# Attention with top-32 selection and an ELU feed-forward: the first batch in single-tile blocks, and another order of the last queries in odd batches

## The chip, the cores and the metric

The kernel runs on one core of a Trainium2 chip. The metric is device time in microseconds (us) of one launch. Before the change, three runs took 1779.0, 1779.35 and 1781.24 us; the median is 1779.35. The engines are named as in the profile: PE is TensorE (matmuls and transposes), DVE is VectorE, ACT is ScalarE, POOL is GpSimd, SP issues the DMAs.

## The reference

There are 8 batches, 8 heads, 576 positions and 64 numbers per head. For each query the 32 largest scores are kept, a softmax is taken over them, and the result weighs the values. The output of all heads, 512 numbers per token for 4608 tokens, then goes through two matrices with an ELU between them.

```python
scores = scale * np.matmul(q, k.transpose(0, 1, 3, 2))
kth = np.partition(scores, -top_k, axis=-1)[..., -top_k:-top_k + 1]   # top_k = 32
mask = scores >= kth
scores = np.where(mask, scores, -1000000000.0)
attn = np.exp(scores - scores.max(-1, keepdims=True))
attn = attn / (attn.sum(-1, keepdims=True) + 1e-09)
x = np.matmul(attn, v)            # (B,H,S,D) -> (B*S, H*D) = 4608 x 512
h = x @ w_in                      # 512 x 2048
g = np.where(h > 0.0, h, np.exp(np.minimum(h, 0.0)) - 1.0)
return g @ w_out                  # 2048 x 512
```

The two weight matrices arrive as 64-bit floats and are turned into 32-bit ones on the chip. Everything else is in 32-bit floats.

## The kernel before, in words

**Tiles and steps.** The 576 queries of a batch are four tiles of 128 queries (numbers 0 to 3) and a rest of 64 (number 4, `J` in the code). A step treats one tile for one head pair, that is 128 queries of two heads. The rest takes four heads in one step, so that its 64 queries still fill 128 rows. A batch is 16 + 2 = 18 steps, and 8 batches are 144 steps. Lines 540 to 549 lay down the order: `order` lists which tiles go together (`(0, 1)` alternates tiles 0 and 1 for each head pair). Even batches go (0,1), (2,3), rest; odd batches go (0,1), rest, (2,3). In the first batch tiles 0 and 1 go singly.

**A step's work.** `scores` (line 274) multiplies keys and queries on PE, and ACT copies the result out. `select` and, for the first eight steps, `select_row` find the 32nd largest score on DVE with eight MAX8 and six MATCH_REPLACE8 per step. `mask` runs Prelu and Exp on ACT, with two small POOL operations before them; `normalise` has a reciprocal on DVE and two multiplications on POOL. `turn` transposes the weights on PE (nine transposes) and ACT copies them out as `et`. Once all tiles of a group are turned, `attend` (line 393) multiplies them with the values: for a pair of tiles 10 matmuls of 256 columns, for one tile 10 of 128, for the rest 20 of 64. `finish` copies the result into the transposed input `xT` of the feed-forward stage.

**The pipeline.** The loop of line 610 spreads a tile's work over steps. In iteration n it emits the scores of step n+2, the selection of n, the mask of n-1, the turning of n-2, and the attend of a group closed one iteration before. From step 8 on the instructions of PE, ACT, DVE and POOL stand in the order written (`manual_schedule`, line 636); before that, and always for SP's DMAs, a scheduler orders them. PE, ACT and DVE each take their instructions in that order.

**Keys, queries and values.** `load_qk` loads two heads' keys and queries, `transpose_qk` turns them with ten transposes on PE and three copies on ACT into `kqT`, and `load_v` loads the values. `ld` has two buffers for keys and two for queries; `kqT` and the values have five each, so a new batch takes over buffers of the old one one by one. Lines 561 to 568 say how many steps before (or, with a minus, after) the batch's first step `f` each of the four head pairs is loaded, turned, and its values loaded. For every batch that is `(7,5,2), (5,3,-2), (3,1,-2), (1,-1,-3)`.

**Feed-forward blocks.** Tokens are gathered into blocks over a pair of batches, nine tile slots in all, where the two rests of 64 share a slot. `division` (lines 517 to 519) gives the blocks: in the first pair (0), (1), (2,3), (rest), (4,5), (6,7), with numbers from 4 on for the odd batch; in later pairs (0,1), (2,3), (rest,4,5), (6,7). When a block's tokens are complete, `ffn_pieces` appends 16 hidden pieces (four matmuls each, then Relu and Exp on ACT, and a gate on DVE that makes the ELU) and four projection pieces for each slot (four matmuls of 512 columns each; the last also copies the result out and stores it). Hidden results pass through two buffers of PSUM, so the third waits for the first one's gate.

**Pacing.** `feed` (line 572) is called four times a step. It hands out pieces from the list in order, at a rate such that the work of all blocks known earlier is done when the next block becomes due. `due` (lines 547 to 554) holds each block's time of readiness, 2.5 steps after its last step, and the work of the blocks before it, in the planner's costs: `HIDDEN` is 1.1, 1.85 or 2.7 per hidden piece of one, two or three slots, `PROJECT` is 3.55 per projection piece. Pieces of later blocks wait until all weights are converted. `hook` (line 189) does a piece of the conversion at each call, four times in each of the first eight steps, and opens the pools `g` and `x` after the last piece. `x` holds `xT` of single-slot blocks from then on, with one buffer.

Of the kernel before, what the change touches and what calls it, by code (L numbers as in the profile page):

```python
# [80 lines left out]
def kernel(  # L81
# [13 lines left out]
    J = S // P  # L95
# [28 lines left out]
    late = {}  # L124
# [64 lines left out]
    def hook():  # L189

        if not decode:
            return
        decode.pop(0)()
        if not decode:
            raws.close()
            late["g"] = ctx.enter_context(tc.tile_pool(name="g", bufs=2))
            late["x"] = ctx.enter_context(tc.tile_pool(name="x", bufs=1))

    def decode_piece(i):
        if i < 2 * NF:  # L200
# [96 lines left out]
    def select_row(u, i):  # L297
        if i == 0:
            u.first = small.tile([P, 2, 8], FP32, tag="m1", name="m1")
            u.last = small.tile([P, 2, 8], FP32, tag="m4", name="m4")  # L300
        sc = u.sc[:, i, :]
        m = u.first[:, i, :]
        nc.vector.max(m, sc)
        wk = wkpool.tile([P, S], FP32, tag=f"wk{i}", name="wk")
        cur = sc
        for r in range(TOP_K // 8 - 1):
            nc.vector.match_replace(wk[:], m, cur, TAKEN)  # L307
            cur = wk[:]
            if r < TOP_K // 8 - 2:
                m = small.tile([P, 8], FP32, tag=f"m{i}", name="m")[:]  # L310
            else:
                m = u.last[:, i, :]
            nc.vector.max(m, cur)  # L313
            if r != 1:
                hook()
                yield

    def select(u):

        u.first = small.tile([P, 2, 8], FP32, tag="m1", name="m1")  # L320
        u.last = small.tile([P, 2, 8], FP32, tag="m4", name="m4")
        cur = [u.sc[:, i, :] for i in range(2)]
        found = [u.first[:, i, :] for i in range(2)]
        for i in range(2):
            nc.vector.max(found[i], cur[i])  # L325
        yield
        wk = [wkpool.tile([P, S], FP32, tag=f"wk{i}", name="wk")[:] for i in range(2)]
        for r in range(TOP_K // 8 - 1):
            for i in range(2):
                nc.vector.match_replace(wk[i], found[i], cur[i], TAKEN)  # L330
            cur = wk
            for i in range(2):
                if r < TOP_K // 8 - 2:
                    found[i] = small.tile([P, 8], FP32, tag=f"m{i}", name="m")[:]
                else:
                    found[i] = u.last[:, i, :]
                nc.vector.max(found[i], cur[i])  # L337
            hook()
            yield
# [174 lines left out]
    for b in range(B):  # L514
        if b % 2 == 0:
            rest = 2 * J
            division = [(0,), (1,), (2, 3), (rest,), (4, 5), (6, 7)]
            if b > 0:
                division = [(0, 1), (2, 3), (rest, 4, 5), (6, 7)]
            slots = {}  # L520
            for part in division:
                blk = Block(len(blocks), len(part))
                blocks.append(blk)
                slots.update((x, (blk, s)) for s, x in enumerate(part))
        first[b] = len(steps)
        tiles = []
        for qt in range(J + 1):
            r0 = b * S + (JP if qt == J else qt)
            if qt == J:
                (blk, slot), c0, n = slots[rest], (b % 2) * R, R  # L530
                rows = slice(r0, r0 + R)
            else:
                (blk, slot), c0, n = slots[(b % 2) * J + qt], 0, P
                rows = slice(r0, r0 + J * (P - 1) + 1, J)
            c0 += slot * P
            t = Tile(b, qt, rows, blk, slice(c0, c0 + n))
            blk.left += NHP
            blk.tiles[slot].append(t)
            tiles.append(t)
        order = [(0, 1), (2, 3), (J,)] if b % 2 == 0 else [(0, 1), (J,), (2, 3)]  # L540
        if b == 0:
            order[:1] = [(0,), (1,)]
        for qts in order:
            for hp in range(NHP // 2 if qts == (J,) else NHP):
                group = Group([tiles[qt] for qt in qts], hp)
                steps += [Step(tiles[qt], hp, group, i) for i, qt in enumerate(qts)]
            for qt in qts:
                n = len(steps)
                tiles[qt].block.ready = n + 1.0 if n <= tight else n + 2.5
# [8 lines left out]
    def at(step, fn, *args):  # L558
        todo.setdefault(step, []).append((fn, args))

    for b in range(1, B):
        f = first[b]
        for hp, (ahead, ready, late_v) in enumerate(
            ((7, 5, 2), (5, 3, -2), (3, 1, -2), (1, -1, -3))
        ):
            at(f - ahead, load_qk, b, hp)
            at(f - ready, start_qk, b, hp)
            at(f - late_v, load_v, b, hp)
# [36 lines left out]
    def step(n):  # L605
        return steps[n] if 0 <= n < NS else None

    closing = []
    main, rest, other = slice(0, J), slice(J, J + 1), slice(J + 1, 2 * J + 1)
    for n in range(NS + 3):  # L610
        for fn, args in todo.pop(n, []):
            fn(*args)
        ahead, cur, prev, done = step(n + 2), step(n), step(n - 1), step(n - 2)
# [86 lines left out]
```

## Time and profile before

| | before |
|---|---|
| median of three runs | 1779.35 us |
| profiled execution, its time | 1779.21 us |
| profiled execution, its span | 1777.4 us |
| PE busy | 1645.8 us (93%) |
| weight loads (PEld, beside PE) | 1014.2 us (57%) |
| DVE busy | 1549.9 us (87%) |
| ACT busy | 1140.0 us (64%) |
| POOL busy | 407.9 us (23%) |
| DMA | 56.19 MB, mean 32 GB/s |
| mean granted PE clock | 0.969 |

The span is the time from the first to the last instruction of the program, and the run's own time is 1.8 us longer. A matmul of the program shows as two MATMUL records, a transpose as one. Busy time on PE includes the tail of a pipelined matmul. The steps can be found in the trace by DVE's first MAX8 on new scores: step 8 starts at 144.22 us, step 20 at 267.89, step 36 at 436.52, step 72 at 844.27, step 140 at 1629.37, and the last, 143, at 1670.34.

### The profile page before, as it was taken

To read this page: it belongs to the slowest core of one execution; us is meant where nothing else is said; L and a number is where in the kernel's file an instruction comes from. 1 tells how busy PE (TensorE), PEld (TensorE's weight loads), DVE (VectorE), ACT (ScalarE), POOL (GpSimd) and SP (SyncE) were. 2 spreads that over 40 slices of the span, in tenths; PEclk is the share of its full clock that TensorE was granted. 3 is DMA by queue.
4 is the path that set the end of the run, shared out by engine and by line. 5 is a ranking of instruction groups with operands and counts; after the bars stand their busy time and mean duration, and the time that the engine had idled before them with its cause. 6 is when DMAs were issued, how large, how long until landed. Compare 5 with 4: busy or idle time off the path is not lost.

```text
span 1777.4 us, 25611 instructions
## 1 busy us (share of the span) xinstructions
PE 1645.8 (93%) x8352; PEld 1014.2 (57%) x8352; DVE 1549.9 (87%) x3376; ACT 1140.0 (64%) x2473; POOL 407.9 (23%) x1078
## 2 busy tenths in 40 slices
PE   5577899999899999999999999999999999999999
PEld 3354656475665666555556565655547475655565
DVE  7999999999899999988999898988889988997700
ACT  6785767676676766667666665756657575756521
POOL 3663222222222222221222122221222211221200
PEclk7568999999999999999999999999999999999999
DMA  6540011001100111001100011001110010000000
GB/s 169 169 131 25 20 47 28 13 18 44 34 7 7 33 34 33 3 19 33 47 12 1 26 38 43 1 13 41 26 27 7 12 29 27 7 6 7 7 13 12
DMA packets 101125, 56.19 MB, mean 32 GB/s; under 512 B 84096, under 2 KB 92288, under 8 KB 100992
## 3 DMA queue, kind: packets, MB, share of 16 engines
q1 hardware_dynamic: 100992, 54.55, 11.1%
q8 instruction: 67, 1.10, 0.3%
q14 instruction: 66, 0.54, 0.1%
HBM read 45.09 MB, written 9.44 MB: 31 GB/s over the span
## 4 chain that ended last, share of the span: by engine, by line
PE 64%; DVE 24%; ACT 6%; issue 2%; DMA 1%; POOL 1%; SPq 0%; ACTq 0%; POOLq 0%
PE ops L485 26%; PE hps L467 17%; DVE wk L330 9%; PE avps L410 8%; DVE m L337 8%; PE scps L285 7%; PE eps L383 5%; DVE m L325 2%; DVE gT L447 2%; ACT et L384 2%; DVE wk L307 1%; DVE m L313 1%; DMA raw<-in_moe_w_in_dram 1%; ACT n L476 1%; ACT n L475 1%
## 5 line engine op out<-in xcount | busy, mean ns | idle before, releaser
L467 PE MATMUL hps<-xT,w_in 128*128 128x256 f32 (+2 forms) x2304 | 563.2, 391 | 27.0 <-DVE gT L447 26.7
L337 DVE MAX8 m<-wk 128x8 f32<-128x576 f32 x816 | 575.8, 747 | 0.0
L485 PE MATMUL ops<-w_out,gT 128*128 128x512 f32 x1152 | 524.8, 600 | 0.6 <-DVE gT L447 0.6
L467 PEld LDWEIGHTS hps<-xT,w_in 128*128 128x128 f32 x2304 | 402.3, 194 | 127.4 <-DVE gT L447 36.0
L330 DVE MATCH_REPLACE8 wk<-m,wk 128x576 f32<-128x576 f32 x544 | 400.0, 743 | 0.0
L485 PEld LDWEIGHTS ops<-w_out,gT 128*128 128x128 f32 x1152 | 209.7, 191 | 221.0 <-issue 215.7
L363 POOL TENSOR_SCALAR dene<-den 128x2 f32<-128x2 f32 x144 | 32.8, 228 | 1062.1 <-ACT sc L354 1061.8
L383 PE MATMUL eps<-ident,sc 128*128 128x128 f32 x1296 | 209.7, 285 | 64.9 <-ACT et L384 33.1
L384 ACT COPY et<-eps 128x512 f32<-128x512 f32 (+1 forms) x432 | 191.0, 473 | 117.1 <-PE eps L383 116.5
L293 ACT ACTIVATE sc<-scps 128x576 f32<-128x576 f32 x288 | 171.9, 648 | 133.5 <-PE scps L285 132.9
L367 POOL TENSOR_SCALAR sc<-sc,rec 128x576 f32<-128x576 f32 x288 | 215.0, 757 | 172.8 <-DVE rec L365 145.3
L383 PEld LDWEIGHTS eps<-ident,sc 128*128 128x128 f32 x1296 | 157.6, 144 | 157.0 <-issue 73.3
L354 ACT ACTIVATE sc<-sc,gap 128x576 f32<-128x576 f32 x288 | 223.2, 775 | 25.2
L353 ACT ACTIVATE sc<-sc,neg 128x576 f32<-128x576 f32 x288 | 223.9, 778 | 22.6 <-POOL neg L350 22.5
L285 PE MATMUL scps<-kqT 64*128 64x512 f32 (+3 forms) x1280 | 203.6, 450 | 12.2 <-ACT sc L293 10.7
L475 ACT ACTIVATE n<-hps 128x256 f32<-128x256 f32 (+2 forms) x288 | 109.1, 379 | 163.9 <-PE hps L467 160.0
L410 PE MATMUL avps<-et,vT 128*64 128x256 f32 (+5 forms) x2000 | 201.5, 337 | 4.0 <-ACT et L384 3.9
L330 DVE MATCH_REPLACE8 wk<-m,sc 128x576 f32<-128x576 f32 x272 | 200.0, 743 | 0.0
L447 DVE SCALAR_TENSOR_TENSOR gT<-n,hps 128x256 f32<-128x256 f32 (+2 forms) x288 | 117.1, 408 | 91.1 <-ACT n L476 90.2
L325 DVE MAX8 m<-sc 128x8 f32<-128x576 f32 x272 | 191.4, 745 | 0.0
L285 PEld LDWEIGHTS scps<-kqT 64*128 64x128 f32 (+1 forms) x1280 | 108.8, 180 | 125.6 <-issue 102.8
L410 PEld LDWEIGHTS avps<-et,vT 128*64 128x64 f32 (+1 forms) x2000 | 113.0, 140 | 90.6 <-issue 50.4
(40 smaller groups left out, 834.5 us busy)
## 6 DMA issues: line engine op xcount, KB each, us to landing
kin<-in_k_dram SPq DMA_DIRECT2D x64, 128.0 KB, 2.8
qin<-in_q_dram SPq DMA_DIRECT2D x64, 128.0 KB, 2.7
raw<-in_moe_w_in_dram SPq DMA_DIRECT2D x16, 512.0 KB, 4.3
vT<-in_v_dram SPq DMA_DIRECT2D x64, 128.0 KB, 2.3
raw<-in_moe_w_out_dram SPq DMA_DIRECT2D x16, 512.0 KB, 3.3
out_dram<-osb SPq DMA_DIRECT2D x32, 256.0 KB, 2.2
kin<-in_k_dram SPq DMA_DIRECT2D x32, 32.0 KB, 2.5
qin<-in_q_dram SPq DMA_DIRECT2D x32, 32.0 KB, 2.5
```

The source lines that it names most:

```text
L285: nc.tensor.matmul(ps[rows, start[i] : start[i] + keys.stop - keys.start], kq[part, 1, q0 : q0 + u.t.ql], kq[part, 0, keys], start=True, s ...
L325: nc.vector.max(found[i], cur[i])
L330: nc.vector.match_replace(wk[i], found[i], cur[i], TAKEN)
L337: nc.vector.max(found[i], cur[i])
L353: nc.scalar.activation(sc, sc, AF.Prelu, bias=neg[:], alpha=STEEP)
L354: nc.scalar.activation(sc, sc, AF.Exp, bias=gap[:], accum_out=u.den[:, i : i + 1])
L367: nc.gpsimd.tensor_scalar(u.sc[:, i, :], u.sc[:, i, :], rec[:, i : i + 1], 1.0, ALU.mult, ALU.mult)
L383: nc.tensor.transpose(ps[:, c * P : (c + 1) * P], sc[:, c0 : c0 + P], ident[:])
L384: nc.scalar.copy(g.et[:, chunks, u.at, :], ps[:, 0 : n * P].rearrange("p (c q) -> p c q", c=n),)
L410: nc.tensor.matmul(ps[i * D : (i + 1) * D, cols], vt[rows, 2 * J if c == J else i * J + c, :], w, start=(c == 0), stop=(c == J),)
L467: nc.tensor.matmul(ps[:, 0:n_tok], w_in[:, i, f * P : (f + 1) * P], blk.xT[:, i, 0:n_tok], start=(i == 0), stop=(i == NC - 1),)
L485: nc.tensor.matmul(blk.o[:], blk.gT[f // NG][:, f % NG, s * P : (s + 1) * P], w_out[:, f, :], start=(f == 0), stop=(f == NF - 1),)
```

## The change

It has four parts. In the first pair of batches the block (2,3) becomes two blocks of one slot, (2) and (3), and tiles 2 and 3 of the first batch go one after the other, as tiles 0 and 1 do. In every odd batch the rest comes first, straight behind the rest of the even batch, so that the two rests of a pair stand in four consecutive steps. Because such a step needs two head pairs, the odd batches' keys and queries are loaded and turned on four consecutive steps before `f`, and their values later. The pool `x` gets a second buffer.

```diff
@@ hook
-            late["x"] = ctx.enter_context(tc.tile_pool(name="x", bufs=1))
+            late["x"] = ctx.enter_context(tc.tile_pool(name="x", bufs=2))
@@ blocks of a pair of batches
-            division = [(0,), (1,), (2, 3), (rest,), (4, 5), (6, 7)]
+            division = [(0,), (1,), (2,), (3,), (rest,), (4, 5), (6, 7)]
             if b > 0:
                 division = [(0, 1), (2, 3), (rest, 4, 5), (6, 7)]
@@ order of the steps
-        order = [(0, 1), (2, 3), (J,)] if b % 2 == 0 else [(0, 1), (J,), (2, 3)]
+        order = [(0, 1), (2, 3), (J,)] if b % 2 == 0 else [(J,), (0, 1), (2, 3)]
         if b == 0:
-            order[:1] = [(0,), (1,)]
+            order[:2] = [(0,), (1,), (2,), (3,)]
@@ loads and transposes of a batch
     for b in range(1, B):
         f = first[b]
-        for hp, (ahead, ready, late_v) in enumerate(
-            ((7, 5, 2), (5, 3, -2), (3, 1, -2), (1, -1, -3))
-        ):
+        plan = ((7, 5, 2), (5, 3, -2), (3, 1, -2), (1, -1, -3))
+        if b % 2 == 1:
+            plan = ((7, 5, 0), (6, 4, -2), (5, 3, -3), (4, 2, -3))
+        for hp, (ahead, ready, late_v) in enumerate(plan):
             at(f - ahead, load_qk, b, hp)
             at(f - ready, start_qk, b, hp)
             at(f - late_v, load_v, b, hp)
```

## The prediction

> **What bounds the kernel now.** I read the page's slices first, then its chain, then the busy time of stretches cut at step boundaries. A step is one of 144 (query tile, head pair) units; its boundary is the first MAX8 of its scores on DVE.
>
> Slices of the span, 44 us each: PE, DVE and the granted TensorE clock.
>
> ```profile
> PE   5577899999899999999999999999999999999999
> DVE  7999999999899999988999898988889988997700
> PEclk7568999999999999999999999999999999999999
> ```
>
> DVE is full from the start and idle in the last two slices; PE has holes only in the first five, where its clock is also often halved. The chain agrees, and its last pieces show what the end consists of:
>
> ```profile
> PE 64%; DVE 24%; ACT 6%; issue 2%; DMA 1%; POOL 1%; SPq 0%; ACTq 0%; POOLq 0%
> ...
> 1718.42 27.63 PE hps L467 x128
> 1746.05 27.48 PE ops L485 x64
> ```
>
> These two are also prices. A matmul is two records, so a 256-column hidden matmul costs 27.63/64 = 0.432 us and a projection matmul 27.48/32 = 0.859.
>
> Busy time by stretch (start:end, length, then PE, PEld, DVE, ACT, POOL, clock, DMA). Rows two to five are steps 8-19, 20-35, 36-71 and 72-139.
>
> ```profile
> 0.00:144.22 144.22, 91.30 (x416) 58.50 (x417) 124.12 (x242) 108.42 (x226) 83.31 (x120) 0.67 0.52 152
> 144.22:267.89 123.67, 105.38 (x650) 68.10 (x648) 122.60 (x279) 82.42 (x191) 28.03 (x82) 0.97 0.10 24
> 267.89:436.52 168.63, 159.85 (x888) 102.09 (x887) 165.25 (x368) 116.72 (x255) 37.78 (x112) 1.00 0.09 23
> 436.52:844.27 407.75, 389.27 (x2078) 245.39 (x2077) 377.82 (x836) 274.59 (x605) 85.34 (x253) 1.00 0.09 23
> 844.27:1629.37 785.10, 757.49 (x3812) 458.62 (x3811) 708.65 (x1549) 505.62 (x1085) 160.39 (x477) 1.00 0.08 21
> 1629.37:1777.43 148.06, 142.51 (x517) 81.53 (x515) 51.40 (x113) 52.27 (x114) 13.08 (x37) 1.00 0.03 9
> ```
>
> Steps 8-19 are DVE's (122.6 of 123.7); PE idles 18.3 us. From step 36 on PE sets the pace, with 3.5 to 4.5% of idle time between its dependent pieces. So the time is PE's work plus PE's idle time. The change can only win by putting feed-forward work (hidden, projection) into the idle 18.3 us.
>
> **What the Trainium skill says.** "Perfetto Trace Analysis", Identifying the Most-Contended Engine, warns that matmul busy time is a poor measure of distance from the limit. I use it only to compare two orders of nearly the same matmuls. "TensorE: Matmul & The Clock Gate", Part 1, says the array runs at half clock until a window of some 3.4 us was busy. This trace agrees: the mean grant is 0.67 before step 8 and 1.00 from step 20. The same page (Architectural detail) says ACT and DVE are strict first-in first-out. That is seen here where PE waits for a copy queued behind a mask:
>
> ```profile
> 1252.99 0.77 ACT L354 ACTIVATE sc<-sc,gap 128x576 f32<-128x576 f32 x1
> 1253.77 0.56 ACT L248 COPY kqT<-qkps 128x512 f32<-128x512 f32 x1
> 1254.47 0.45 PE L383 MATMUL eps<-ident,sc 128*128 128x128 f32 x1 [2.45 <-ACT kqT L248]
> ```
>
> **The change, part by part.** Its instruction lists are fixed before it runs, so I count them by step and multiply by prices fitted to PE's busy time over the steps from 22 on: hidden 0.244 / 0.441 / 0.672 us for 128 / 256 / 384 columns, projection 0.875, attend 0.26 (256) and 0.092 (64), the rest about 2.5 per step. They give 390.4 for steps 36-71, where the row shows 389.3. DVE prices are starts from one instruction to the next: MAX8 0.663, MATCH_REPLACE8 with its load 0.727, gate 0.204 / 0.32 / 0.471.
>
> 1. *Block (2,3) split.* 128 narrow hidden matmuls for 64 wide: 128x0.244 - 64x0.441 = +3.0 us. 80 narrow attend matmuls for 40 wide: at 0.15 each (half of the wide 0.26 is the floor; the measured 0.26 of the narrow ones, 16.8 us for 131 records, is partly at half clock and the ceiling) 12.0 - 10.4 = +1.6, bounds 0 and +10. Gates: 32x0.204 - 16x0.32 = +1.4 of DVE.
> 2. *Earlier work.* The pacing spreads the work known to be due. With (2), (3) and the last queries due at steps 14.5, 18.5 and 22.5 instead of 18.5 and 30.5, feed-forward work is 20 us ahead by step 20. But the same pacing gives it back: 17 us ahead after step 39, 3.0 us (just the split's cost) by step 65, and what is left from step 140 on is the same (127.8 us in both). The lead never reaches the tail.
> 3. *Sums by stage.* PE before/after: 105.1/123.6, 161.5/161.3, 390.4/374.8, 751.8/751.8, end 152.0/152.0. DVE: 122.8/124.3, 165.1/167.4, 375.7/372.5, 703.6/703.6. Measured time over the larger sum before: 1.007, 1.021, 1.045, 1.044. Steps 8-19 come into balance, so I take 1.034 there, a little above the 1.021 of the balanced steps 20-35, for the narrow gates' latency: 124.3x1.034 = 128.5, +4.8. Steps 20-35: 167.4x1.021 = 170.9, +2.3. Steps 36-71: 374.8x1.045 = 391.7, -16.1.
> 4. *Odd batches, last queries first.* Scores, transposes and attends move, their number stays; PE's sum for steps 72-139 is unchanged. But four head pairs are turned in four consecutive steps, and the scores of the second step need the pair turned just before: they wait for two ACT copies (0.57 and 0.27), possibly behind a pair of hidden activations (0.38 and 0.42), while PE has about 0.8 of its own (six transposes at 0.11 and the first score matmul). An estimate of 0.9 us for each of three odd batches, +2.7 (bounds 0, and 7.4 for the 2.45 seen above). In the first odd batch DVE covers it. Behind that matmul stand the step's attend and transposes, and behind those ACT's mask and DVE's reciprocal.
> 5. *DMAs.* The same transfers. Keys and queries are asked for two steps ahead of their transposes; 2.8 us to land against 20. The third pair's load waits for the first pair's transposes, still two steps early. Values land 2.3 us after the attend that frees their buffer, a step (10 us) before use. Next-batch key loads stand ahead of them in SP's queue, but wait for earlier transposes. Uncovered, each would cost 2.3-2.8. The second xT buffer costs nothing; without it (3) would wait for (2)'s hidden stage.
> 6. *Steps 0-7.* Same chain of decode and selection; step 6 gets 2.9 us more hidden work at a partly halved clock: +1 (0 to 4; a gain of 3 if the clock rises sooner).
>
> Sum: +4.8 +2.3 -16.1 +2.7 +1 = -5.3. The profiled run took 1779.21 for a span of 1777.4; 1777.4 - 5.3 + 1.8 = 1773.9, and the median stands 0.1 above that run: **1774**.
>
> **Rivals.**
> *A, likeliest (0.47): as summed,* 1774, own range 1766 to 1775.8. For it: in steps 41-49, where the sums nearly agree (93.0 PE, 92.6 DVE), the trace needs 93.4, so PE's backlog carries over steps.
> *B (0.20): the gain is eaten.* The stall in part 4 takes 2.45 us and the narrow stage 0.2 us a step more: within 0.2%, 1779. Narrow hidden work does cost idle time before: over steps 37-39, all of it narrow, 36 us hold 3.6 of PE waiting for gates,
>
> ```profile
> L467 PE MATMUL hps<-xT,w_in 128*128 128x128 f32 x128 | 16.7, 281 | 3.6 <-DVE gT L447 3.6
> ```
>
> *C (0.26): slower, no carry.* If every step lasts as long as the larger of its own two sums, steps 8-139 go from 1476.4 to 1482.1: +10.1 in 8-19, +0.4 in 20-35, -7.1 in 36-71, +2.2 after; with parts 4 and 6, +9.4: 1789. For it: the step-wise sums of before fit 36-71 as well (408.3 against 407.8). Against: they give 173.2 for steps 20-35, which took 168.6. It decides from the point where 36-71 give back less than about 7 us instead of 16.
> *D (0.07): full carry,* the early steps cost only 2 and 36-71 give 20: 1766 or less.
> That the change does nothing is excluded: the lists differ from step 6 on.
>
> **How the numbers follow.** A measurement of this kernel tells 0.2% (3.6 us) from no change. A and D are faster, 0.54; B same, 0.20; C slower, 0.26. For 8 in 10 the range leaves out the lower half of D and the upper half of C: 1763 to 1788.
>
> **What would show it.** Right: steps 8-19 at 127-130 us with PE idle below 8; steps 36-71 at 388-396; steps 72-139 within 5 of 785; the last 148 us unchanged; a wait of the score matmuls for kqT's copy once per odd batch, near 1 us. Wrong: DVE idle above 6 us in steps 8-28 waiting for hidden activations (C), or the score wait above 2 us (B).

## The result, and the profile after

The changed kernel takes 1783.09 us (median of 20 runs, 1780.95 to 1784.88); the kernel before, run beside it on the same chip, takes 1779.41. The ratio is 1.0019, with a 95% interval of 1.0012 to 1.0026. So the change costs 3.7 us, 0.2%, where 5.3 us less were forecast. The profiled execution of the change has a span of 1779.9 us against 1777.4, 2.5 us more.

First the page's slices of the span again (44.5 us each: PE and the granted PE clock, in tenths).

```profile
PE   5577999999999999999999999999899999999999
PEclk8569999999999999999999999999999999999999
```

PE's row is at 9 from the fifth slice on, but for one 8 far behind; before, its fifth and eleventh slices were at 8. This fits work that was brought forward; the table by stretch below shows it. The chain of work that ended last is nearly the old one (PE has 65% of it and DVE 23%, where they had 64 and 24), and it ends with the same last pieces, 27.63 and 27.48 us long, 2.5 us later.

```profile
1720.87 27.63 PE hps L467 x128
1748.50 27.48 PE ops L485 x64
```

The busy time by stretch, cut at the same steps (start to step 8, steps 8-19, 20-35, 36-71, 72-139, the last four; columns: start:end, length, PE, PEld, DVE, ACT, POOL, clock, DMA share, GB/s), shows where the time went.

```profile
0.00:149.16 149.16, 92.12 (x441) 61.74 (x442) 124.54 (x246) 110.47 (x236) 82.44 (x122) 0.72 0.50 147
149.16:283.02 133.86, 120.35 (x851) 80.67 (x850) 125.08 (x288) 86.19 (x214) 27.49 (x79) 0.99 0.11 27
283.02:455.30 172.28, 159.03 (x1000) 110.07 (x999) 167.97 (x386) 122.63 (x292) 37.77 (x112) 1.00 0.08 19
455.30:849.12 393.82, 374.63 (x1947) 230.07 (x1945) 374.08 (x821) 266.94 (x572) 85.33 (x253) 1.00 0.09 24
849.12:1631.73 782.61, 757.20 (x3812) 456.77 (x3811) 708.71 (x1548) 504.95 (x1085) 160.41 (x477) 1.00 0.08 21
1631.73:1779.90 148.17, 142.57 (x517) 81.44 (x515) 51.71 (x113) 52.56 (x114) 13.09 (x37) 1.00 0.03 9
```

Steps 36-71 do get 13.9 us shorter (407.75 to 393.82). But steps 8-19 get 10.2 longer (123.67 to 133.86), steps 20-35 3.7 and the steps before 8 4.9. Together steps 8-71 take 699.96 us where they took 700.05. The lead (the feed-forward work brought forward) was paid for, almost to the last tenth, before it paid back. What is left of the difference is the 4.9 us ahead of step 8, less 2.5 in steps 72-139. In steps 8-19 DVE was full before and now stands still for 8.8 us. Its waits in that stretch of the change (what waited, for what, us in all, times, longest):

```profile
DVE rec L365 <- POOL dene L363: 4.5, 2, 2.4
DVE gT L447 <- ACT n L476: 4.1, 9, 0.9
```

Before, the same two rows read 0.3 and 0.8 us. (Some expectations below give 6.2 us for the second row. That figure includes one wait of 2.04 us that ended at 148.95 us, ahead of step 8, and so belongs to step 7.) PE is not full either: it idles 13.5 of 133.9 us, 8.7 of them waiting for gates (shown with e13 below). On the page, hidden matmuls wait 35.3 us for gates over the whole program, where they waited 26.7:

```profile
L467 PE MATMUL hps<-xT,w_in 128*128 128x256 f32 (+2 forms) x2432 | 563.1, 378 | 37.6 <-DVE gT L447 35.3
```

And in the narrow steps 10-12 (33.0 us) the row that the prediction showed for three narrow steps of before, with 3.6 us of waiting, has 6.5:

```profile
L467 PE MATMUL hps<-xT,w_in 128*128 128x128 f32 x128 | 17.4, 283 | 6.5 <-DVE gT L447 4.6 <-ACT xT L437 1.8
```

How a load on PE reaches DVE is seen in the timeline of step 14 (start, length, engine, line, operation; in brackets the idle time before it and what ended it):

```profile
217.85 3.70 PE L485 MATMUL ops<-w_out,gT 128*128 128x512 f32 x8
...
221.39 0.71 PE L383 MATMUL eps<-ident,sc 128*128 128x128 f32 x5
...
222.03 0.75 ACT L384 COPY et<-eps 128x512 f32<-128x512 f32 x2 [2.56 <-PE eps L383]
...
222.67 0.79 ACT L353 ACTIVATE sc<-sc,neg 128x576 f32<-128x576 f32 x1
...
224.50 0.23 POOL L363 TENSOR_SCALAR dene<-den 128x2 f32<-128x2 f32 x1 [9.51 <-ACT sc L354]
224.76 0.17 DVE L365 RECIPROCAL rec<-dene 128x2 f32<-128x2 f32 x1 [2.45 <-POOL dene L363]
```

A projection piece (3.70 us) stands on PE ahead of the transposes `eps`. ACT waits 2.56 us for these, because their copies `et` come next in its queue. Behind the copies stands the second head's mask, behind the mask POOL's sum, and behind that DVE's reciprocal, which waits 2.45 us. DVE has the next step's first MAX8 ready, but behind the reciprocal. So a peak on PE makes DVE wait within the same step. Whether such a wait costs the kernel time is another question, which e11 answers.

### The profile page after: what moved, and what is told of

Same layout as the page of the kernel before. It is cut to its first block, busy times and chain, and to the rows that moved or that the text cites. A ratio compares the mean times of both kernels' runs of the same rounds, so it can differ in the third digit from the quotient of the medians.

```text
span 1779.9 us, 26067 instructions
## 1 busy us (share of the span) xinstructions
PE 1645.9 (92%) x8560; PEld 1020.8 (57%) x8560; DVE 1552.1 (87%) x3392; ACT 1143.7 (64%) x2509; POOL 406.5 (23%) x1078
## 4 chain that ended last, share of the span: by engine, by line
PE 65%; DVE 23%; ACT 7%; issue 2%; POOL 1%; DMA 1%; SPq 0%; ACTq 0%; POOLq 0%
PE ops L485 28%; PE hps L467 16%; DVE wk L330 8%; PE avps L410 8%; DVE m L337 7%; PE scps L285 7%; PE eps L383 5%; DVE gT L447 2%; DVE m L325 2%; ACT et L384 2%; ACT n L476 1%; DVE wk L307 1%; DVE m L313 1%; ACT n L475 1%; ACT sc L353 1%
## 5 line engine op out<-in xcount | busy, mean ns | idle before, releaser
L467 PE MATMUL hps<-xT,w_in 128*128 128x256 f32 (+2 forms) x2432 | 563.1, 378 | 37.6 <-DVE gT L447 35.3
L467 PEld LDWEIGHTS hps<-xT,w_in 128*128 128x128 f32 x2432 | 408.4, 193 | 135.0 <-DVE gT L447 47.3
L367 POOL TENSOR_SCALAR sc<-sc,rec 128x576 f32<-128x576 f32 x288 | 215.1, 757 | 150.1 <-DVE rec L365 133.7
L285 PE MATMUL scps<-kqT 64*128 64x64 f32 (+3 forms) x1280 | 204.0, 451 | 11.5 <-ACT sc L293 10.0
L285 PEld LDWEIGHTS scps<-kqT 64*128 64x128 f32 (+1 forms) x1280 | 105.4, 181 | 127.7 <-issue 104.1
```

The lines of the kernel that those rows point to most:

```text
L285: nc.tensor.matmul(ps[rows, start[i] : start[i] + keys.stop - keys.start], kq[part, 1, q0 : q0 + u.t.ql], kq[part, 0, keys], start=True, s ...
L367: nc.gpsimd.tensor_scalar(u.sc[:, i, :], u.sc[:, i, :], rec[:, i : i + 1], 1.0, ALU.mult, ALU.mult)
L467: nc.tensor.matmul(ps[:, 0:n_tok], w_in[:, i, f * P : (f + 1) * P], blk.xT[:, i, 0:n_tok], start=(i == 0), stop=(i == NC - 1),)
```

## The experiments

All comparisons are with the kernel before, run beside each. Stage times below are of one profiled execution each; stages whose instructions are the same in two kernels agreed within 0.2 us (steps 20-35 and 72-139 of the change and of e13), only the time to the first step (15.2 to 16.6) scatters. The profiled execution need not be the median one: e2's took 1.2 us more than the median, e4's 2.8 more, e8's 8.9 less. A step begins with an instruction of DVE, so an edit that moves work in DVE's queue can move a boundary without a gain. The table gathers them (us; "0-7" are the first eight steps).

```
                           0-7   8-19  20-35  36-71  72-139  last   ratio and 95% interval
before                    129.1  123.7  168.6  407.8  785.1  148.1
change                    132.8  133.9  172.3  393.8  782.6  148.2  1.0019 (1.0012-1.0026)
e1_split                  129.2  127.9  166.4  411.1  784.9  152.4  1.0058 (1.0046-1.0071)
e2_rest_first             129.2  124.4  177.4  400.8  786.2  148.1  1.0022 (1.0016-1.0029)
e3_narrow                 129.2  122.8  171.6  407.9  786.1  148.1  1.0017 (1.0010-1.0023)
e4_old_pace               128.8  123.2  175.0  411.7  781.1  150.5  1.0029 (1.0019-1.0039)
e5_mask_first             132.9  136.0  178.1  410.5  843.0  152.1  1.0497 (1.0483-1.0511)
e6_mask_first_before      129.5  128.0  181.1  431.6  839.1  150.6  1.0542 (1.0523-1.0560)
e7_late_lead              128.2  135.9  174.0  399.1  785.3  147.3  1.0041 (1.0029-1.0054)
e8_both                   128.4  141.3  185.7  415.8  839.2  149.9  1.0609 (1.0595-1.0624)
e9_ease                   129.8  133.7  176.3  397.8  785.9  148.1  1.0050 (1.0038-1.0063)
e10_ease_few              131.6  138.8  175.8  397.9  786.4  147.3  1.0075 (1.0061-1.0088)
e11_late_rec              133.0  131.2  174.4  395.5  782.2  148.2  1.0020 (1.0011-1.0028)
e12_late_rec_before       128.0  122.4  166.1  411.4  785.0  148.1  1.0003 (0.9995-1.0012)
e13_short_select          132.2  129.6  172.3  392.2  782.6  148.2  0.9957 (0.9940-0.9974)
e14_short_select_before   129.6  112.3  168.6  408.5  785.1  148.0  0.9937 (0.9922-0.9951)
e15_ease_short_select     129.0  125.2  177.1  397.5  786.0  148.1  1.0008 (1.0000-1.0017)
```

### The parts alone

**The split alone** (e1), the last queries in the old order, with three buffers in `x` for the narrow blocks' `xT`:

```
-            division = [(0,), (1,), (2, 3), (rest,), (4, 5), (6, 7)]
+            division = [(0,), (1,), (2,), (3,), (rest,), (4, 5), (6, 7)]
-            order[:1] = [(0,), (1,)]
+            order[:2] = [(0,), (1,), (2,), (3,)]
```

> The split alone: blocks (2) and (3), tiles 2 and 3 one after the other, the rest of odd batches where it was (the x pool has three buffers, since the block of the rest now waits longer with its xT open). If the peaks of PE inside steps 8-19 are the cost (theory S), these steps, whose larger sums by step are 127.9 against 123.4 before and 133.5 with the whole change, take about 128; steps 36-71 give nothing back (PE's sum is 390.4 as before), and the run is 4 to 7 us slower than before. If the narrow pieces' latency is the cost (N), steps 8-19 take 131 or more here too. If the rest-first order is the cost (R), this run is not slower than before by more than the split's own 4.6 us of PE work.

It took 1790.71 us, about 11 more than before and more than was expected (S had 4 to 7). Theory R falls with it: without the new order of the last queries this is the slower kernel. Steps 8-19 cost 4.2 of the 11. Steps 36-71 give nothing back (+3.3; PE's busy time in steps 36-53 stays at 193.9 us, 194.3 before). And the last four steps cost 4.3 us, all of it in the first three of them, where PE is busy 2.2 us longer (with 9 more records) and idles 3.2 us of 45.3 (1.1 of 41.0 before). A likely cause, only argued: pieces are handed out by a running sum, so one more or less early on shifts where all later ones fall within their steps.

**The order of the last queries alone** (e2), with its plan of loads, and the old blocks:

```
-        order = [(0, 1), (2, 3), (J,)] if b % 2 == 0 else [(0, 1), (J,), (2, 3)]
+        order = [(0, 1), (2, 3), (J,)] if b % 2 == 0 else [(J,), (0, 1), (2, 3)]
+        if b % 2 == 1:
+            plan = ((7, 5, 0), (6, 4, -2), (5, 3, -3), (4, 2, -3))
```

> The order of the rest alone: odd batches begin with it, with the new plan of loads, and the blocks are as before. R expects it slower by 3 us or more, with steps 72-139 longer by 3 or more than before. S and N expect steps 8-19 within 1 us of before (larger sums 124.0), steps 20-35 up by 3 to 5 (PE's sum 166.8 against 161.5), steps 36-71 down by 6 to 7 (PE's sum 383.5 against 390.4), and the run within 3 us of before.

It took 1783.06 us, 3.7 more. The block of the last queries is ready eight steps earlier, so its work is brought into steps 20-35, which get 8.8 us longer (3 to 5 were expected); steps 36-71 get 7.0 shorter, and 72-139 take about 1 more (R had 3 or more). This is the pattern of the whole change on a smaller scale: paid in one stage, given back in the next, a little less.

**The narrow blocks alone** (e3): the new `division`, the old order of tiles, so that (2) and (3) are ready hardly earlier than the pair was; `x` has three buffers.

```
-            division = [(0,), (1,), (2, 3), (rest,), (4, 5), (6, 7)]
+            division = [(0,), (1,), (2,), (3,), (rest,), (4, 5), (6, 7)]
```

> The narrow blocks without their earlier readiness: (2) and (3) are blocks of one slot, but tiles 2 and 3 alternate as before and both blocks become due at step 18.5; x has three buffers. The lead is thus not taken. By the counts it adds 3.0 us of PE work and 1.4 of DVE. S expects 2 to 5 us over before, steps 8-19 within 1 us of before. N expects 7 or more, with PE waiting longer for gates in steps 18-30.

It took 1782.81 us, 3.5 more, 3.0 of it in steps 20-35, where the narrow blocks are worked off. This is the price of the split itself, within S's 2 to 5 us and below N's 7; the prediction's part 1 had +4.6 of PE and +1.4 of DVE for it.

**The whole change without the lead** (e4): the blocks' due times in the first pair are set back to the old ones, and `x` has three buffers.

```
+                if b == 0 and qt == 2:
+                    tiles[qt].block.ready = 18.5
+                if b == 1 and qt == J:
+                    tiles[qt].block.ready = 30.5
```

> The whole change, but block (2) is given the due time 18.5 and the block of the rest 30.5, so that the first pair is paced as before (x has three buffers). The lead of 20 us by step 20 is gone (the feed-forward work by step 20 is 65 us against 85 with the change and 66 before). If the lead is what pays in steps 36-71, these are longer than before by 5 to 10 (PE's sum 400.2 against 390.4), steps 0-19 last as before, and the run is slower than the whole change by 5 or more. If the lead is what costs, this run is faster than the whole change by 5 or more.

Steps 8-19 return to 123.2 us and 36-71 to 411.7. This kernel still turns the keys in four steps on end, and it has 199 records of narrow hidden matmuls in steps 8-19 (151 before, 256 in the change). So it is the lead, not the narrow shapes as such nor the bunched turning of keys, that makes steps 8-19 longer, and the lead that makes 36-71 shorter. Over the whole program it is worth little: 1785.0 us without it, 1783.09 with it, with intervals that overlap; 5 us or more were expected, one way or the other.

### The order of ACT's queue

The timeline above suggests to put the second head's mask ahead of the transposes' copies. e5 does that in the change, e6 in the kernel before.

```
+        if prev:
+            mask(prev, 1)
         if done:
             turn(done, main)
             turn(done, rest)
-        if prev:
-            mask(prev, 1)
```

> The whole change, and in each step from 8 on the mask of the second head (Prelu and Exp on ACT) is emitted ahead of the two copies of turned weights instead of behind them. The work and its order on PE and DVE are the same. Theory Q: a backlog of PE reaches DVE within the same step, because the mask queues on ACT behind copies that wait for PE, and DVE's reciprocal waits for the mask; so peaks of PE add to the time even where the sums balance. Q expects DVE's waits for the reciprocal to fall to below 1 us in steps 8-19 (4.5 with the change), these steps to fall from 133.9 to 127-131, and the run to be 3 to 10 us faster than with the change alone. If the narrow pieces' latency is the cost (N), steps 8-19 stay above 132 and the waits for hidden activations (6.2) remain or grow.

> The kernel before with the same earlier mask. Q expects steps 8-19 unchanged (123.7: DVE has no idle time there), and in steps 36-139, where PE sets the pace, a gain only of what PE itself waited: the run 0 to 5 us faster than before. The difference between the run with the change and this one is then the price of the change with backlog allowed: Q expects 0 to 5 us faster with the change, where it is 3.7 us slower without the earlier mask.

Both lose some 5%, and theory Q falls. DVE's wait for the reciprocal in steps 8-19 does fall, from 4.5 to 2.6 us, but its waits for activations there rise from 4.1 to 8.3, and now PE waits for the copies behind the mask. PE's waits for them over the whole program, of the change and then of e5:

```profile
PE eps L383 <- ACT et L384: 28.9, 43, 1.1
```

```profile
PE eps L383 <- ACT et L384: 105.8, 84, 3.7
```

The wait was not removed, it went to the engine that sets the pace later: 60 of the 85 us that e5 loses against the change lie in steps 72-139. e5 is 7.6 us faster than e6, so in that order the change would win.

### Where the lead is taken

**The lead only from step 8 on** (e7): the old due times hold until then.

```
+    slow = [due[0], due[1], (18.5, due[2][1])]
...
+        known = slow if n < tight else due
+        ahead = [(w - fed["sum"]) / (x - fed["at"]) for x, w in known if x > fed["at"]]
```

> The whole change, but up to step 8 the feed-forward work is paced as before, so that the lead is gathered only afterwards. If the faster pace in steps 0-7 is what made step 7 take 19.2 us instead of 16.1, steps 0-7 are back at 129 (132.8 with the change). The step-wise larger sums are then 132.1 in steps 8-19 and 170.4 in steps 20-35 (133.5 and 173.6 with the change), PE's sum in 36-71 is 3.5 higher. Together 2 to 6 us faster than the change. If step 7 was an accident of the clock, steps 0-7 stay near 132.

Steps 0-7 return to 128.2 us, so their +3.7 in the change came from the faster pace. But the whole, 1787.1 us, is 4 us slower than the change, not faster: what is left out of steps 0-7 comes in steps 8-19 (135.9) and later.

**Both** (e8):

> The late lead and the earlier mask together on the whole change. If both causes are right and add up, 5 to 12 us faster than the change, and below the kernel before.

At 1886.7 us, nothing is gained from the combination; steps 20-35 are at their longest here, 185.7.

**The feed cut where it peaks.** By then the lengthening of steps 8-19 fitted one rule: every step lasts as long as the larger of its own sums on PE and DVE. Sum and time were 123.4 and 123.7 before, 133.5 and 133.9 in the change, 127.9 and 127.9 in e1, 124.0 and 124.4 in e2. If so, levelling the peaks should win the stage back. e9 and e10 multiply the share that `feed` adds in some steps:

```
+EASE = {7: 0.7, 8: 0.6, 13: 0.7, 14: 0.7, 15: 0.8, 16: 0.8, 18: 0.9, 19: 0.8, 20: 0.8}
-            fed["over"] += max(0.0, share * min(ahead))
+            fed["over"] += max(0.0, share * min(ahead)) * EASE.get(n, 1.0)
```

> The whole change, with the feed of hidden and projection work cut at the steps where it peaks: the share of the work due that a step takes is multiplied by 0.7, 0.6, 0.7, 0.7, 0.8, 0.8, 0.9, 0.8, 0.8 in steps 7, 8, 13, 14, 15, 16, 18, 19, 20. By step 20 the feed-forward work stands at 78 us (change 85, kernel before 66); what is left out there comes later, so the PE sum of steps 36-71 is 381.8 (change 374.8, before 390.4). Theory S (in steps 8-19 every step lasts as long as the larger of its own PE and DVE sums, so it is the peaks inside the stage that cost the 10 us): larger sums by step 127.7, so steps 8-19 take 127 to 129.5 (change 133.9), step 7 takes 16 to 17 (change 19.2); steps 20-35 as in the change, 172 to 175. Steps 36-71: 381.8 x 1.045 = 399 if the total of PE decides there, 403.6 if the larger sums by step do. The whole then lies 2 to 5 us below the change, about 1779 to 1781. Theory N (the narrow blocks' latency or the amount of work brought forward costs the time, whatever its division over steps): steps 8-19 stay at 132 or more, and the whole is 3 to 6 us above the change.

> The whole change with the feed cut harder at fewer steps (factors 0.5, 0.6, 0.6, 0.8, 0.8 in steps 8, 13, 14, 18, 20). Sums nearly those of the other eased kernel for steps 8-19 (larger sums by step 127.5, PE 116.6) and the same PE sum for steps 36-71 (381.8), but there the larger sums by step are 407.1 instead of 403.6. Theory S: steps 8-19 take 127 to 129.5. For steps 36-71 it tells two rules apart: if PE's total decides (backlog carried over steps), both eased kernels take the same there, about 399; if the larger sums by step decide, this one takes 3 to 4 us more than the other (407 against 404). Theory N: steps 8-19 at 132 or more.

The rule fell. Both kernels are slower than the change, and steps 8-19 take 133.7 and 138.8 us where it gives 127.7 and 127.5; e7 had already missed it by 3.8. Why it fitted the four earlier kernels is not known. In steps 36-71, on the other hand, the eased kernels take 397.8 and 397.9 us: the same PE sum (381.8), but larger sums by step of 403.6 and 407.1. There PE's total decides, as the prediction's case A had it (381.8 x 1.045 = 399.0).

The granted clock may have a part in the loss, but that is not shown. Its mean in steps 8-19 is 0.97 in e9 and 0.96 in e10, against 0.99 in the change; but it is 0.96 in e1 too, which took no longer than its sum, and 0.97 in the kernel before.

### DVE's waits, and what each engine needs alone

**The reciprocal moved** behind the next step's first MAX8 pair, in the change (e11) and in the kernel before (e12). The next mask's two small POOL instructions are put ahead of it (`edges`).

```
         next(passes)
+        if prev:
+            edges(prev, 0)
+        if done:
+            normalise(done)
         feed(n, 0.25)
...
-        if prev:
-            normalise(prev)
```

> The whole change, with one thing moved: the reciprocal of a step's denominators stands in DVE's queue behind the next step's first two MAX8 (1.4 us of work) instead of ahead of them, and the next mask's two small POOL instructions stand ahead of it in POOL's queue. Same instructions, same feed. Theory W (the 10 us of steps 8-19 are DVE's own waits in its queue, 4.5 us for reciprocals behind late masks and 6.2 us for gates behind late activations, each of which can be taken away by itself): the reciprocal waits fall from 4.5 to under 1.5 us, steps 8-19 take 129.5 to 131.5 instead of 133.9; later stages gain at most a few us, since PE sets the pace there although DVE waits 10.7 us for reciprocals in steps 36-71 and 50.8 in steps 72-139; the whole lies 3 to 10 us below the change, 1773 to 1780. Theory P (PE's work and its own waits, 120.3 + 13.5 us, fill the stage, and DVE's waits only show that it runs ahead of PE): the waits move to the gates or to the next reciprocal, steps 8-19 stay within 1.5 of 133.9 and the whole within 3 us of the change.

> The kernel before with the same move of the reciprocal. Steps 8-19 have 0.3 us of such waits before, so under both theories they stay at 123 to 124.5. Theory W: steps 36-71 (16.5 us of reciprocal waits, 407.8) and 72-139 (52.6 us, 785.1) gain where DVE's waits come back to PE: 2 to 5 us and 3 to 8 us. Theory P: no stage moves by more than 2 us, the whole within 3 us of the kernel before.

DVE's waits in steps 8-19 of e11:

```profile
DVE gT L457 <- ACT n L486: 5.1, 9, 2.2
DVE rec L375 <- POOL dene L373: 1.1, 1, 1.1
```

The reciprocals wait 1.1 us instead of 4.5, the gates 5.1 instead of 4.1, and the stage takes 131.2 instead of 133.9, as theory W has it. But this is a moved boundary and no gain. In the change a wait of 2.0 us for step 19's reciprocal ends just ahead of step 20; in e11 this reciprocal stands behind step 20's first MAX8, so that step 20 begins earlier and the wait falls into the next stage. Step 8 starts 0.4 us later in e11 than in the change, and step 21 still 0.3 us later (293.71 against 293.37). Steps 20-35 take 2.1 us more, 36-71 1.7 more, and the whole comes to 1783.33 us, the time of the change. In the kernel before, the same move takes reciprocal waits in steps 72-139 from 52.6 to 27.5 us and gate waits there from 23.1 to 48.9, and the whole stays the same (1779.62 us); there too, steps 20-35 (-2.5) and 36-71 (+3.7) change by more than the whole. So theory P holds: DVE's waits show that it has run ahead of PE, and to remove one moves it.

**DVE's load taken away.** e13 to e15 leave one of the three rounds of MATCH_REPLACE8 and MAX8 out of the selection in steps 8-19 and 36-53 (so 24 scores are taken there and the output differs), in the change, the kernel before and the eased change (e9). PE's instructions are untouched. The first line below stands for both loops of a round.

```
+            for i in range(0 if short and r == 1 else 2):
-        passes = select(cur) if cur else iter(range(4))
+        passes = select(cur, 8 <= n < 20 or 36 <= n < 54) if cur else iter(range(4))
```

> The whole change, with one of the three rounds of MATCH_REPLACE8 and MAX8 left out of the selection in steps 8-19 and 36-53 (24 instead of 32 scores are taken there, so the output differs): DVE has 2.8 us less to do in each of these steps, its sum in steps 8-19 is 91.0 instead of 124.3; PE's list is untouched (123.6). Theory P (PE's work with its own dependent waits fills steps 8-19 of the change): the stage stays at 131 to 134. Theory K (coupling: neither engine fills it, each waits for the other in turns): it falls to 123 to 128. In steps 36-53 (194.5 in the change, PE busy 185.5) P gives 192 to 194.5, K 187 to 190.

> The kernel before with the same round left out of steps 8-19 and 36-53. Steps 8-19 lose their bound (DVE 122.8 to 89.5, PE 105.1): both theories let them fall, P to 113 to 116 (PE's sum with the 8 per cent of waits that the change shows there), K to 106 to 110. Steps 36-53 (202.0, PE busy 194.3): P 200 to 202, K 195 to 198.

> The eased change with the same round left out of steps 8-19 and 36-53. PE's sum in steps 8-19 is 116.6. If PE's work and its waits set the 133.7 us of the eased kernel there (P), it stays above 130; if the coupling does (K), it falls to 117 to 122, that is about 7 us below the change with the same round left out, as the sums stand.

Steps 8-19 in the busy time by stretch, first of e13 (change), then e14 (before), then e15 (eased):

```profile
147.66:277.26 129.60, 119.84 (x851) 80.66 (x850) 92.69 (x215) 85.75 (x214) 27.36 (x79) 0.99 0.11 28
```

```profile
145.48:257.75 112.27, 100.45 (x650) 66.46 (x648) 90.16 (x207) 81.47 (x191) 27.91 (x82) 1.00 0.11 27
```

```profile
144.52:269.74 125.22, 113.33 (x838) 79.67 (x838) 92.93 (x217) 87.83 (x219) 28.67 (x82) 0.98 0.12 29
```

With 32 us less to do on DVE, the change's steps 8-19 still take 129.6 us. That is at most what PE needs there by itself: 119.8 of busy time and 9.8 of waits. In the kernel before, PE by itself needs 112.3, and DVE's 122.6 of work covered it. So the change's 133.9 us is made of two terms. The lead raises PE's own pace by 17.3 us, past DVE's 125, to 129.6. And with DVE's whole load beside it the stage takes 4.3 us more. PE's waits in steps 8-19, first of the change, then of e13, show where these are:

```profile
PE hps L467 <- DVE gT L447: 8.7, 7, 1.8
PE eps L383 <- ACT et L384: 3.0, 5, 0.7
PE hps L467 <- ACT xT L437: 1.8, 1, 1.8
```

```profile
PE hps L467 <- DVE gT L447: 6.1, 5, 1.3
PE eps L383 <- ACT et L384: 2.8, 5, 0.6
PE hps L467 <- ACT xT L437: 0.8, 1, 0.8
```

Hidden matmuls wait 2.6 us less for gates and 1.0 less for a copy of `xT` once DVE has less to do; PE's busy time is 0.5 less. A gate stands in DVE's queue behind a part of the selection: in step 10 of the change PE stands idle for 1.37 us while DVE ends two MAX8, and goes on at 176.82 us, when the gate behind them, begun at 176.50, is done. So a full DVE makes PE's hidden matmuls wait longer. "Coupling" below means this: two engines near their limits, and the slower one waits for the other's queue. The result lies between theories P (131 or more) and K (128 or less). The eased kernel lies between them too: 125.2 with the lighter DVE (P had 130 or more, K 122 or less), and 8.5 more with the whole load. Of these, 3.9 are longer busy time of PE for nearly the same records (117.2 in e9 against 113.3, at a mean clock of 0.97 against 0.98), and the rest are waits of PE that were not followed up.

In steps 36-53 the same cut takes 48 us from DVE and only 3.4 us from the change's 194.5 and 1.5 from the 202.0 before. PE sets the pace there.

No kernel that computes the whole output was shown to be faster than the kernel before.

## Why the prediction was wrong, point by point

The forecast of -5.3 us was the sum of five terms, and the spans show +2.5.

1. *Steps 8-19, part 3: +4.8 forecast, +10.2 measured. This step failed.* It multiplied the larger sum, DVE's 124.3, by 1.034 and expected PE to idle below 8 us. But PE's sum of 123.6, with the factor 1.045 that the prediction itself used for PE where PE paces, is 129.2, and e13 measured 129.6 with a lightened DVE. So the stage was no longer DVE's: the prediction saw equal sums and left out that PE's sum takes PE's waits on top. In size this is only 1.1 us of the miss of 5.4, since 124.3 x 1.034 gave 128.5. The other 4.3 us is the coupling: PE waits longer for gates because DVE is full, for which the factor had almost nothing. The prediction's own example of two nearly equal sums, steps 41-49 before (93.4 us for 93.0 and 92.6), is right, but it spoke for a loss of 0.4%, where 20-35 lost 2% and 8-19 now 8% of the larger sum. Why balance is cheap in one stretch and dear in another stays open.
2. *Steps 20-35: +2.3 forecast, +3.7 measured.* The stage is mis-sized by 1.4 us. It may be the same error, but no run took one engine's load away there.
3. *Steps 36-71: -16.1 forecast, -13.9 measured.* Right in mechanism, and e9, e10 and e13 support it. The measured ratio to PE's sum is 1.051 instead of 1.045, which is the 2.2 us (e9 and e10 had 1.042).
4. *Scores behind the keys' copies, part 4: +2.7 forecast for three odd batches.* The waits of the score matmuls' weight loads for `kqT` over the whole program:

```profile
PEld scps L285 <- ACT kqT L257: 2.8, 4, 0.7
```

These are four waits, one in each odd batch; the kernel before has no such wait. The last three are 0.74 us each, 2.2 together, against 0.9 each forecast. They are waits of the weight loads; PE itself shows no idle time there, since the step's first score matmul runs meanwhile, so they cost less than they last. Case B's stall of 2.45 did not come. Steps 72-139, which hold two of them, got 2.5 us shorter, not longer. That is luck: matmuls last 3.7 us longer there before, in stretches at half clock, and none do in the change (below), which nobody had forecast.
5. *Steps 0-7, part 6: +1 forecast, +3.7 measured,* of which 3.1 in step 7 (a further 1.2 us ahead of step 0 is scatter: e13, with the same instructions there, took 0.9 less than the change). e7 shows that the pace makes it. The cost was taken for the few microseconds of hidden work at a low clock; but at the end of step 7 DVE also waits 2.04 us for an activation, which the prediction had not counted.
6. *The split's own price, part 1, the tail, part 2, and the loads, part 5* held: +3.5 in e3; the last four steps within 0.1 us; waits of PE and its weight loads for keys, queries and values come to 5.8 us over the whole program, 7.7 before. That the tail holds does not follow from an equal amount of work alone: in e1 the last steps took 4.3 us more.

Case C had 8-19 right at +10.1 and predicted +9.4 in all, but by a rule that the eased kernels refute, and it had steps 36-71 at half their gain. Case A had 36-71. The forecast took "balanced" for a state with little loss. It set 8.1 us of cost in steps 0-35 against 16.1 of gain in 36-71; measured are 17.6 against 13.9. From -5.3 to +2.5 are 7.8 us: 5.4 from steps 8-19, 1.4 from 20-35, 2.2 from 36-71 and 3.9 ahead of step 8, less 5.2 in steps 72-139, where +2.7 was set for the odd batches.

One of the signs of being wrong that were named beforehand, DVE idle above 6 us in steps 8-28 waiting for hidden activations, did show: 7.1 us (1.1 before), with 4.5 more for reciprocals. Of the signs of being right, steps 36-71, 72-139, the last 148 us and the score wait held; steps 8-19 (133.9 us, PE idle 13.5) did not.

What stays open: what makes the eased kernels lose so much in steps 8-19; why the same balance costs so little in steps 41-49; and whether the phase of the feed is what costs e1 its tail.

## What to carry to other kernels

"Perfetto Trace Analysis" of the Trainium skill (Optimization Strategy) says that interleaving regimes with different most-contended engines may improve a kernel. Here 18.5 us of PE's work (by the prediction's counts) were brought into a stage in which PE idled 18.3 us, and nothing was won: before filling an engine's idle time, add its own dependent waits (here 5 to 8%) to its sum and compare that with the other engine. Near balance it can take more still (here 4.3 us on 129.6). To learn which engine paces a stage, take the other one's load away and time the stage; a wait alone does not tell, since in e5, e11 and e12 waits that were removed appeared again elsewhere. Cut stages at a mark that the edit does not move, or look one step further: e11's 2.6 us were a moved mark. And time a local edit over the whole program: e1 lost 4.3 us in its last four steps, far from what it changed.

## What the runs showed of the hardware that was not expected

A short pause of PE was sometimes, and not always, followed by half the clock. In the kernel before, PE waits 2.45 us for the `kqT` copy at 1252 us (the wait that the prediction showed). What PE does after the transpose that waited, and the busy time of the 3.4 us from the end of the wait:

```profile
1254.71 4.01 PE L467 MATMUL hps<-xT,w_in 128*128 128x384 f32 x7
```

```profile
1254.47:1257.90 3.43, 3.43 (x6) 1.93 (x7) 3.43 (x8) 2.16 (x5) 0.23 (x1) 0.50 0.00 0
```

The clock is 0.50 for 3.43 us, and seven records of hidden matmuls take 4.01 us. The same happens at 1203 us; in the two bursts the records of matmuls last 3.7 us longer than usual, so about 1.9 us for each. In the change the same wait comes in the same step:

```profile
1257.57 0.30 PE L383 MATMUL eps<-ident,sc 128*128 128x128 f32 x1 [2.45 <-ACT kqT L248]
1257.71 2.75 PE L467 MATMUL hps<-xT,w_in 128*128 128x384 f32 x8
```

```profile
1257.57:1261.00 3.43, 3.43 (x14) 2.25 (x15) 3.43 (x8) 2.64 (x6) 0.23 (x1) 1.00 0.03 7
```

Here the clock stays at 1.00, as it does after waits of 2.45 us at 840 us before and at 845 us in the change. In the 3.41 us up to the end of each of these five waits PE was busy for 0.96 or 0.97 us, so neither the gap nor the work ahead of it tells the two cases apart, and what does is open. The Trainium skill, "TensorE: Matmul & The Clock Gate" (Why this matters for your kernels), asks for no idle gaps above some 3 us between bursts of matmuls; here a gap of 2.45 us was too long twice and harmless three times, and the measurement decides: to stay below 3 us is not always enough. The length of the slow stretch, 3.4 us, is the window that the page states in Part 1.
